# New order lists for the five engines of an adaLN block with infini-attention, on one core

## The chip, the cores and the metric

The kernel runs on one core of a Trainium2 chip. Its engines work side by side: TensorE (PE) multiplies matrices, VectorE (DVE) and ScalarE (ACT) work on tiles and read what PE leaves in PSUM, GpSimd (POOL) works on tiles in SBUF, SyncE (SP) issues nearly all transfers. The metric is the device time of one execution in microseconds (us), the median of several runs. Lower is better. The kernel before runs in 747.37 us (median of 3 runs, 746.82 to 749.26).

## What is computed

The block is a transformer layer in float32 over 2048 positions of width 512: a layer norm modulated by a condition vector, causal attention over four segments of 512 positions with 32 heads of 16, mixed by a gate with a linear memory that is carried from segment to segment, an output projection, a second modulated layer norm, and a dense layer of 1792 with the square of a ReLU.

```python
phi = lambda t: jnp.where(t > 0, t + 1.0, jnp.exp(t))
for s in range(N):                       # 4 segments of 512
    logits = jnp.einsum("bhqd,bhkd->bhqk", qs, ks) * scale + mask
    p = _softmax(logits, axis=-1)
    a_dot = jnp.einsum("bhqk,bhkd->bhqd", p, vs)
    pq = phi(qs)
    num = jnp.einsum("bhld,bhde->bhle", pq, M)
    den = jnp.einsum("bhld,bhd->bhl", pq, z)[..., None] + 1e-6
    o = g * num / den + (1.0 - g) * a_dot
    pk = phi(ks)
    M = M + jnp.einsum("bhld,bhle->bhde", pk, vs)
    z = z + jnp.einsum("bhld->bhd", pk)
...
mod = (_silu(c) @ w_mod).reshape(c.shape[0], 6, 1, -1)
sa, ca, ga, sb, cb, gb = (mod[:, 0], mod[:, 1], mod[:, 2], mod[:, 3], mod[:, 4], mod[:, 5])
h = _layernorm(x, axis=-1) * (1 + ca) + sa
x = x + ga * _A_ref(h, ...)              # attention and the projection wo
h = _layernorm(x, axis=-1) * (1 + cb) + sb
r = relu(h @ w1 + b1)
x = x + gb * ((r * r) @ w2 + b2)
```

## The kernel before

Matrices are held as a high part and a rest, so that a product of float32 accuracy is three products of the faster type. The attention is cut into 16 units: unit u is segment u // 4 and a group of 8 heads, u % 4; each unit is worked in two quads of four heads.

For a unit, PE first makes queries and keys (bqk, L868), and for a segment the values (bv, L938). ACT and DVE split queries and keys in two parts (sg, L899 and L901), and SP copies the parts into the buffer ST by many small transfers, the fills (L917). For each quad PE then makes masked scores (ba, L976) of which DVE takes the row maxima (mx, L981; one reduction, L1020, goes by a copy ac of ACT, L1009). PE turns the maxima (bat, L1041), ACT negates them (mt, L1043), and SP writes them as a further row into ST (two transfers, L1049). Only then can PE make the scores less their maximum (bpb, L1145); ACT takes the exponentials (pt, L1162), POOL masks them, PE multiplies them with the values (bpv, L1204), and at the end of a unit PE turns the results (bfin) and DVE divides them in two halves, each of three instructions (L1253 to L1256, result on). The memory is read on PE (bmr, L1069) and brought up to date by way of bmu and tm (L1106, L1121).

At the end of the attention the blocks of the output weights wo are loaded (L1297, four of 256 KB), multiplied by the gate on DVE (L1298), cast to their high part on ACT (L1299) and split on DVE (L1300). They land in the place of the value weights, so the loads wait for the last value product. The projection starts with a transposition (bwot, L1332).

The dense layer runs both of its products as seven block products each (L1652 the first, L1737 the second). In the first pass p counts pairs of 128-column blocks of w1 and s the segment; its operands come from a transformed w1 in HBM (w1d0 to w1d6) by fetches (L1579) into buffers that the products of an earlier p release.

Nothing of the order is left to a scheduler. The program makes a list of nodes (a node is one step on one engine: a group of matmuls, one copy, one or two transfers), each with its inputs and the buffers that it takes and gives back. `Plan.run` then plays the nodes through a model with a duration for each, and issues them in the order that comes out. On each engine it takes them in the order of a table of node numbers, `ORDER`. PSUM's eight banks and most tiles come from pools in that same play: a node takes the bank that has been free for longest, so another order also changes which earlier user's release a node waits for.

Of the kernel before, what the change touches and what calls it, by code (L numbers as in the profile page):

```python
# [69 lines left out]
1208 1499 1240 1500-1501 1236 1144 1248 1503-1504 1331 1243 1505 1220 1506 1325 1481 1338 1482 1346 1483 1560 1328  # L70
1484 1322 1252-1254 1256 1259 1486 1349 1487 1263 1488 1334 1489 1343 1617 1352 1618 1515 1619-1620 1523 1271 1266
1622-1623 1529 1624 1355 1625 1275-1277 1520 1752 1368 1753 1279 1371 1754 1536 1755 1544 2043 2039 1375 1757 1557
1378 1758 1526 1759 1383 1760 1547 2047 2035 1387 1550 1532 1388 1563 1389 1541 1650 1692 1391 1887 1398 1888 1401
1889 1394 1655 1890 1664 1406 1892 1410 1661 1566 1893 1569 1894 1553 1895 1658 1671 1411-1412 1676 1573 1576 1685
1695 1585 1682 1581 1586 1589 1827 1667 1587 1592 1698 1596 1679 1599 1414 1604 1608 1785 1790 1701 1609 1830 1793
1704 1610 1708 2051 1711 2052 1799 1716 2053 1688 2054 1806 1820 1612 1720 1833 1721-1722 1724 1814 2056 1727 2057
1796 1731 2058 1734 1962 1739 2059 1817 1802 1743-1745 1920 1811 2080-2081 1928 1836 1823 2082 1934 2083 1843 1747
2085 1851 2086 1846 2087-2088 1925 1839 2209-2210 1931 2156 1941 2211-2212 1949 1937 1855-1857 1859 1955 2214 2114
2215 1952 2216 1965 2217 2119 1862 2097-2099 1866 2100 1869 1946 2102 1874 2103 2125 1958 2104 2135 2146 2105 2149
1878 496 1879-1880 1971 2128 2333 1974 2334 1978 2140 2335 2122 2336 1981 1882 2338 1986 2339 2143 2340 2131 2341 2259  # L80
498 1990 2273 1994 1991-1992 1997 2457 2270 2001 2458 2004 2459 2152 2264 2460 2280 2238 2462 2267 2463 2009 2464 2246
2465 2243 2013-2014 2249 2159 2015 2162 2166 2169 2017 1968 2178 2276 2174 2252 2599 2362 2182 2179-2180 2185 2404
2602-2603 2189 2604 2376 2605 2192 2197 2607-2608 2255 2609-2610 2373 2633 2616 2201 2383 2367 2202-2203 2283 2370
2619 2286 2620-2622 2290 2298 2379 2624-2625 2205 2486 2626-2627 2293 2650 2302 2500 2636-2639 2397 2306 2303 2641
2309 2642 2497 2643-2644 2653-2654 2394 2655-2656 2491 2667 2304 2658 2313 2659-2660 2316 2661 2670-2671 2321 2388
2672-2673 2684 2407 2675-2676 2410 2677-2678 2391 2325-2327 2494 2414 2687 2417 2688-2689 2400 2690 2701 2422 2692
2507 2693-2695 2512 2781 2769 2430 2503 2426 2433 2515 2437 2427-2428 2521 2440 2704 2445 2705-2706 2531 2707 2518
2777 2773 2718 2449-2451 2538 2524 2709-2711 2534 2721 2712 2722 2541 2723-2724 2453 2546 2726-2729 2554 2557 2550
2329 2561 2564 2551 2528 2569 2552 2573-2575 2973 2577 2977 2972 2828 2817 2974-2975 2831-2833 2976 2834 2820 2839
2821-2822 2978 2823 2842-2843 2994 2806 2844 2993 2845 2996 2995 2850 2998-2999 2809 2997 2810-2812 2853 2861  # L90
2854-2856 3014-3015 3122 2864 3016 2883 3017 2865-2867 3314 3018 2886 3019 2887 2872 3020 2888-2889 3035-3036 3038
3037 2875-2878 3041 3040 3120 3119 3121 3039 3329 3054 3133 3131 3319 3055 3143 3134 3056 3324 3057 3146 3132 3060
3059 3058 3144 3074-3075 3073 3145 3078 3076 3079 3158 3077 3155 3092 3094-3095 3093 3157 3098 3097 3167 3156 3170
# [1742 lines left out]
```

## Time and profile before

| | before |
|---|---|
| runs | 747.37 us (746.82 to 749.26) |
| profiled execution | 746.45 us |
| its span | 744.7 us |
| TensorE busy | 724.5 us |
| VectorE busy | 623.7 us |
| GpSimd busy | 495.5 us |
| ScalarE busy | 485.7 us |
| transfers over the span | 151.82 MB, mean 204 GB/s |

The profile is one execution. Its span runs from the first instruction to the last; the execution's own time is 1.75 us longer. "Busy" is the time in which an engine has an instruction in work. In rows of waits, the name left of the arrow is the instruction that stood idle, and the one to the right released it. A row of a timeline starts with the start and the duration in us, joins neighbours of one kind (x2, x12), and puts an idle time ahead of it in brackets. SPq is SP's queue of transfers: its rows show how long the issue took, not the transfer. PEclk is the granted clock of TensorE, 1.00 being full speed.

### The profile page before, as it was taken

Reading aid. Unit: us, or ns where it says so; the run is one execution under the profiler, and the core shown is the slowest. Engines: PE = TensorE matmul, PEld = TensorE weight load, DVE = VectorE, ACT = ScalarE, POOL = GpSimd, SP = SyncE. Lnnn points to the kernel's source line nnn. Section 1 sums busy time; section 2 is a strip of 40 time slices with the busy share of each in tenths; the row PEclk is TensorE's granted clock in tenths of the full one; section 3 lists DMA queues with packets and bytes.
Section 4 is the critical chain, followed back from the end, with each engine's and each line's share of the span. In section 5 each row is a group of like instructions: output and inputs, shape, how many; then the busy total and the mean of one; then the engine's idle time right before and its main releaser. Section 6 shows DMA issues by size and latency. Waiting matters only on the chain. (4 is left out here: it accounts for less than half of the span.)

```text
span 744.7 us, 20355 instructions
## 1 busy us (share of the span) xinstructions
PE 724.5 (97%) x7405; PEld 612.3 (82%) x7405; DVE 623.7 (84%) x1674; ACT 485.7 (65%) x1070; POOL 495.5 (67%) x675
## 2 busy tenths in 40 slices
PE   8989999999999999998999999999999999999996
PEld 7876778666767677784777788999999999999996
DVE  6578898898898889888998879789788888777785
ACT  3759887999979987787779645574435443534342
POOL 6767857789858786553996656656666665466572
PEclk9999999999999999999999999999999999999999
DMA  9877874545644363438762897898876678776620
GB/s 310 259 212 236 236 198 115 154 121 165 193 145 121 94 184 96 124 98 270 252 207 88 232 358 255 301 330 290 288 234 218 225 256 263 261 237 223 195 83 29
DMA packets 84606, 151.82 MB, mean 204 GB/s; under 512 B 10134, under 2 KB 32666, under 8 KB 84508
## 3 DMA queue, kind: packets, MB, share of 16 engines
q1 hardware_dynamic: 84356, 150.40, 64.4%
q8 instruction: 59, 0.97, 0.5%
q14 instruction: 39, 0.32, 0.1%
q10 hardware_dynamic: 152, 0.13, 0.1%
HBM read 94.14 MB, written 29.36 MB: 166 GB/s over the span
## 5 line engine op out<-in xcount | busy, mean ns | idle before, releaser
L981 DVE CUSTOM_DVE_ANT_0 ba<-ba,msk 128x384 f32<-128x384 f32 (+2 forms) x384 | 192.9, 531 | 26.9 <-PE ba L976 19.8
L1162 ACT ACTIVATE pt<-bpb 128x512 f32<-128x512 f32 x320 | 173.4, 618 | 10.3 <-PE bpb L1145 8.8
L1149 POOL TENSOR_SCALAR_AFFINE_SELECT pt<-pt 128x512 f32<-128x512 f32 x128 | 80.3, 646 | 52.8 <-ACT pt L1162 38.4
L868 PE MATMUL bqk<-HT,WQK 64*128 64x512 f32 x720 | 105.2, 396 | 0.4 <-ACT HT L844 0.3
L1737 PE MATMUL bm<-w,ST 128*128 128x256 f32 x660 | 93.5, 283 | 0.5 <-DVE ST L1725 0.4
L1737 PEld LDWEIGHTS bm<-w,ST 128*128 128x128 f32 x660 | 85.0, 191 | 1.1 <-DVE ST L1725 1.1
L1652 PE MATMUL bh<-ST 128*128 128x256 f32 x600 | 84.4, 283 | 1.1 <-DMA ST<-w1d 1.1
L1145 PE MATMUL bpb<-ST 64*128 64x256 f32 (+2 forms) x512 | 79.5, 349 | 3.1 <-DMA ST<-mt 2.4
L1204 PE MATMUL bpv<-pt,VT 128*32 128x512 f32 (+3 forms) x1024 | 82.0, 438 | 0.3 <-ACT lnf L657 0.2
L1652 PEld LDWEIGHTS bh<-ST 128*128 128x128 f32 x600 | 77.1, 190 | 2.0 <-ACT H2o L1443 1.3
L868 PEld LDWEIGHTS bqk<-HT,WQK 64*128 64x128 f32 x720 | 70.4, 185 | 9.5 <-ACT VT L944 0.8
L976 PE MATMUL ba<-ST 63*128 63x256 f32 (+2 forms) x512 | 75.2, 341 | 2.0 <-DVE on L1256 1.3
L976 PEld LDWEIGHTS ba<-ST 63*128 63x128 f32 x512 | 50.1, 185 | 21.9 <-DVE mx L981 2.6
L1145 PEld LDWEIGHTS bpb<-ST 64*128 64x128 f32 x512 | 51.6, 188 | 19.9 <-DVE mx L981 3.1
L938 PE MATMUL bv<-WVO,HT 64*128 64x512 f32 x384 | 54.8, 399 | 0.0
L1204 PEld LDWEIGHTS bpv<-pt,VT 128*32 128x32 f32 x1024 | 27.1, 109 | 33.5 <-issue 26.5
L981 DVE DVE_READ_ACCUMULATOR2_ANT mx<- 128x1 f32 x384 | 54.2, 141 | 0.1
L910 POOL TENSOR_SCALAR e<-e 128x512 f32<-128x512 f32 x24 | 35.8, 1493 | 16.4 <-ACT e L906 16.2
L938 PEld LDWEIGHTS bv<-WVO,HT 64*128 64x128 f32 x384 | 38.0, 188 | 4.3
L1009 ACT COPY ac<-ba 128x512 f32<-128x512 f32 x64 | 36.2, 604 | 7.0 <-PE ba L976 6.2
L779 POOL TENSOR_TENSOR X1L<-X1L 128x512 fp32r<-128x512 f32 (+1 forms) x28 | 32.2, 1149 | 12.4 <-ACT X1L L778 12.0
L1020 DVE TENSOR_REDUCE mx<-ac 128x4 f32<-128x1024 f32 x32 | 38.9, 1215 | 0.3 <-POOL ac L1017 0.2
(291 smaller groups left out, 1719.7 us busy)
## 6 DMA issues: line engine op xcount, KB each, us to landing
ST<-sg SPq DMA_DIRECT2D x192, 128.0 KB
ST<-w1d SPq DMA_DIRECT2D x20, 1024.0 KB
ST<-w1d SPq DMA_DIRECT2D x20, 768.0 KB
w1d<-X1L SPq DMA_DIRECT2D x21, 512.0 KB
w1c<-w1d SPq DMA_DIRECT2D x8, 1024.0 KB
w1c<-w1d SPq DMA_DIRECT2D x8, 768.0 KB
xt<-in_A_x SPq DMA_DIRECT2D x16, 256.0 KB
wm<-in_w_mod SPq DMA_DIRECT2D x16, 256.0 KB
```

Source lines behind the costliest of these rows:

```text
L868: nc.tensor.matmul(bank(banks[w]), W3(w, k, x, cols.start, cols.stop)[r], HT[r, y, k], start=first and i == 0, stop=last and i == 2)
L938: nc.tensor.matmul(bank(banks[t]), HT[r, x, k, (t2 + t) * P:(t2 + t + 1) * P], WVO[r, k, y], start=first and i == 0, stop=last and i == 2)
L976: nc.tensor.matmul(dst[:, c0:c0 + n], ST[b:b + 63, 0, sl, qt * P:(qt + 1) * P], ST[b:b + 63, 1, sl, :n], start=True, stop=True)
L981: nc.vector.tensor_tensor_reduce(i, i, msk[:, 512 - n:], scale=1.0, scalar=-3e38, op0=ALU.add, op1=ALU.max, accum_out=o)
L1009: cp = [act(512, lambda j=j: nc.scalar.copy(buf("ac", ac)[:, j], bank(keys[j])), pr[0] + 0.01 + 0.001 * j, after=[first], put=[keys[j]]) f ...
L1020: reds.append(op("DVE", 1.13, lambda: nc.vector.tensor_reduce(buf("mx", mx).rearrange("p (a t) -> p a t", t=4)[:, :, 1], acv(), axis=AX.X, ...
L1145: nc.tensor.matmul(dst, ST[b:b + 64, 1, sl, kb * P:(kb + 1) * P], ST[b:b + 64, 0, sl, q0:512], start=True, stop=True)
L1149: nc.gpsimd.affine_select(out=ap, in_=ap, pattern=[[0, ap.shape[1]], [1, P]], compare_op=ALU.is_ge, fill=0.0, base=0, channel_multiplier=-1)
L1162: ns = [op("ACT", 0.49, lambda j=j: nc.scalar.activation(buf("PPP"[n], pt)[:, i + j], bank(keys[j]), AF.Exp, scale=0.25), pr[slot] + 0.01 ...
L1204: nc.tensor.matmul(bank(o)[32 * hq:32 * hq + 32, q0:q0 + src.shape[1]], v[:, a:a + 32], src, start=start, stop=stop, tile_position=(0, 32 ...
L1652: nc.tensor.matmul(pb(i), A[:, x, kk], B[:, y, kk], start=kk == j == 0, stop=kk == 1 and j == 2)
L1737: nc.tensor.matmul(q if wide else q[:, c * HALF:(c + 1) * HALF], TL[ao][a >= 3][:, x, a_ * P:(a_ + 1) * P], LT["w2z"][:, b:15:14 - b] if w ...
```

## The change

Only the table `ORDER` is different: the five lists hold the same node numbers (1309 for PE, 1054 for ACT, 984 for DVE, 617 for POOL, 499 for SP) in another order, found by a search, stretch by stretch, over six draws of durations, transfer landings and queue rate. No node, duration, pool or line of code is changed besides. The first lines of PE's list stand for all:

```diff
     "PE": """
-8-24 3 25-33 56 34-37 58 64 38-39 82 78 66 90 40-43 86 44-47 252 246-249 253-255 405-408 410-413 291-293 308 294 322
-564-565 319 296 316 297 566 313 567 298-299 329 569-570 337 571 325 572 340 274-275 334 276-277 350 355 279 362 365
...
+8-24 3 25-33 56 34-37 58 64 38-39 82 78 66 90 40-43 86 44-47 252-253 246-247 254 248-249 255 405-408 410 291 411-413
+292-293 308 322 294 564-565 316 296 313 297 566-567 319 298-299 329 569-570 337 325 571-572 340 274-277 334 350 355
...
```

Three places show what that moves. The first is the head of the attention, the first row of maxima of unit 0. SP's list before, from the two clears of ST (L749) to the transfers of that row (L1049); wm is a load of the modulation's weights:

```order
L781 DMA w1d_131<-X1L 256x2x256
L917 DMA ST<-sg 32x2x512 x3
L749 DMA ST<-pad 32x4x512 x2
L917 DMA ST<-sg 32x2x512
L590 DMA wm<-in_w_mod 128x512
L917 DMA ST<-sg 32x2x512
L1049 DMA ST<-mt 1x8x128 x2
L917 DMA ST<-sg 32x2x512
```

and now:

```order
L781 DMA w1d_131<-X1L 256x2x256
L917 DMA ST<-sg 32x2x512 x3
L749 DMA ST<-pad 32x4x512 x2
L917 DMA ST<-sg 32x2x512
L1049 DMA ST<-mt 1x8x128 x2
L917 DMA ST<-sg 32x2x512
L781 DMA w1d_131<-X1L 256x1x256
L917 DMA ST<-sg 32x2x512 x6
```

The load of w_mod and one fill between the clears and the row have gone behind it. On PE the same place before, from the masked scores (ba) to the first scores (bpb); the number behind ba is its bank's tile:

```order
L976 MATMUL ba_643<-ST 128x384
L976 MATMUL ba_644<-ST 128x384
L868 MATMUL bqk<-HT,WQK 128x512 x6
L1041 MATMUL bat<-ident,mx 16x64 x2
L868 MATMUL bqk<-HT,WQK 128x512 x6
L976 MATMUL ba_683<-ST 128x512
L976 MATMUL ba_684<-ST 128x512
L938 MATMUL bv<-WVO,HT 128x512 x12
L976 MATMUL ba_711<-ST 128x512
L976 MATMUL ba_712<-ST 128x512
L938 MATMUL bv<-WVO,HT 128x512 x12
L1094 MATMUL bpkt<-ident,phi_469 128x64 x8
L1145 MATMUL bpb<-ST 128x512 x2
```

and now:

```order
L976 MATMUL ba_645<-ST 128x384
L976 MATMUL ba_646<-ST 128x384
L1041 MATMUL bat<-ident,mx 16x64 x2
L868 MATMUL bqk<-HT,WQK 128x512 x12
L976 MATMUL ba_682<-ST 128x512
L976 MATMUL ba_683<-ST 128x512
L938 MATMUL bv<-WVO,HT 128x512 x24
L976 MATMUL ba_733<-ST 128x512
L976 MATMUL ba_734<-ST 128x512
L1094 MATMUL bpkt<-ident,phi_411 128x64 x8
L1145 MATMUL bpb<-ST 128x512 x2
```

The transposition of the maxima (bat) stands ahead of one group of six products of bqk that was ahead of it before, and one pair of masked scores has moved behind all the value products.

The second place is the scaling of the output weights, in units 11 to 14. DVE before (numbers tell the tiles apart; wo_6304, wo_6321 and wo_6329 are the first three blocks in the order of their loads, bfin and on belong to unit 11, tm to its memory):

```order
L1020 TENSOR_REDUCE mx_6281<-ac_6220 128x4
L1298 TENSOR_TENSOR wo_6329<-wo_6329,gab_6082 128x512
L1121 TENSOR_TENSOR tm_6423<-bmu_6397,bdm_101 128x34
L1298 TENSOR_TENSOR wo_6321<-wo_6321,gab_6082 128x512
L1253 RECIPROCAL bfin_6373<-bfin_6373 128x16
L1255 TENSOR_TENSOR dn_6434<-bfin_6373,omg_77 128x16
L1256 TENSOR_TENSOR on_6437<-bfin_6373,dn_6434 128x4x64
L1253 RECIPROCAL bfin_6375<-bfin_6375 128x16
L1255 TENSOR_TENSOR dn_6448<-bfin_6375,omg_77 128x16
L1256 TENSOR_TENSOR on_6437<-bfin_6375,dn_6448 128x4x64
L1298 TENSOR_TENSOR wo_6304<-wo_6304,gab_6082 128x512
```

and now (the first three blocks loaded are wo_6293, wo_6306 and wo_6321):

```order
L1298 TENSOR_TENSOR wo_6293<-wo_6293,gab_6076 128x512
L1298 TENSOR_TENSOR wo_6306<-wo_6306,gab_6076 128x512
L1253 RECIPROCAL bfin_6368<-bfin_6368 128x16
L1255 TENSOR_TENSOR dn_6400<-bfin_6368,omg_77 128x16
L1256 TENSOR_TENSOR on_6403<-bfin_6368,dn_6400 128x4x64
L1298 TENSOR_TENSOR wo_6321<-wo_6321,gab_6076 128x512
L1121 TENSOR_TENSOR tm_6434<-bmu_6406,bdm_101 128x34
L1020 TENSOR_REDUCE mx_6283<-ac_6222 128x4
L1253 RECIPROCAL bfin_6366<-bfin_6366 128x16
L1255 TENSOR_TENSOR dn_6461<-bfin_6366,omg_77 128x16
L1256 TENSOR_TENSOR on_6403<-bfin_6366,dn_6461 128x4x64
```

Two scalings and one half of a unit's end stand ahead of tm now, and the reduction, which was ahead of all, has moved behind tm. SP before, from the fills ahead of the loads on:

```order
L1049 DMA ST<-mt 1x8x128 x2
L917 DMA ST<-sg 32x2x512 x6
L1297 DMA wo<-in_A_wo 128x512
L1522 DMA T_6297<-gb_dram 128x512
L1297 DMA wo<-in_A_wo 128x512 x2
L917 DMA ST<-sg 32x2x512
L1321 DMA ot<-o_dram 128x512
L1322 DMA xw<-in_A_x 128x512
L917 DMA ST<-sg 32x2x512 x4
L1297 DMA wo<-in_A_wo 128x512
```

and now:

```order
L1049 DMA ST<-mt 1x8x128 x2
L917 DMA ST<-sg 32x2x512 x4
L1297 DMA wo<-in_A_wo 128x512 x3
L1321 DMA ot<-o_dram 128x512
L1322 DMA xw<-in_A_x 128x512
L917 DMA ST<-sg 32x2x512 x2
L1297 DMA wo<-in_A_wo 128x512
```

The first three loads of wo follow one another, with four fills instead of six between them and the row of maxima ahead, and the load T<-gb_dram is no longer among them. Of the fills of unit 14, eight instead of seven stand ahead of the loads in all.

The third place is the end of the dense layer's first pass over segment 0. SP before; w1d_136 and w1d_137 are the blocks for p = 5 and p = 6, L1374 stores rows of the sum behind the attention, L1690 partial sums of the dense layer, L1693 loads such sums again:

```order
L1579 DMA ST<-w1d_136 128x2x1024
L1693 DMA Tx_7999<-xs_146 128x512
L1579 DMA ST<-w1d_136 128x2x768
L1579 DMA w1c<-w1d_137 128x2x1024
L1690 DMA xs_148<-T_6297 128x512
L1374 DMA x_dram<-Tx_8001 128x512
L1579 DMA ST<-w1d_137 128x2x768
L1579 DMA ST<-w1d_131 128x2x1024
```

and now:

```order
L1579 DMA ST<-w1d_136 128x2x1024
L1374 DMA x_dram<-T_6303 128x512
L1579 DMA ST<-w1d_136 128x2x768
L1579 DMA w1c<-w1d_137 128x2x1024
L1374 DMA x_dram<-X1L 128x512
L1579 DMA ST<-w1d_137 128x2x768
L1579 DMA ST<-w1d_131 128x2x1024
L1596 DMA w_8795<-w2d_144 128x1792
```

A store (L1690) has moved from between the fetches of p = 6 to behind them, a load (L1693) from between those of p = 5. PE before, the products of p = 5 (six to a group) from the first that reads the second half's operands:

```order
L1737 MATMUL bm<-w_7992,ST 128x256 x6
L1652 MATMUL bh<-H2o_6295,ST 128x256 x6
L1652 MATMUL bh<-ST 128x256 x6
L1652 MATMUL bh<-H2o_6294,ST 128x256 x6
L1737 MATMUL bm<-w_7992,ST 128x256 x6
L1652 MATMUL bh<-ST 128x256 x18
L1737 MATMUL bm<-w_7993,ao 128x256 x3
L1652 MATMUL bh<-ST 128x256 x6
```

and now:

```order
L1737 MATMUL bm<-w_7999,ST 128x256 x9
L1652 MATMUL bh<-H2o_6301,ST 128x256 x6
L1652 MATMUL bh<-H2o_6300,ST 128x256 x6
L1652 MATMUL bh<-ST 128x256 x24
L1737 MATMUL bm<-w_7999,ST 128x256 x6
L1652 MATMUL bh<-ST 128x256 x6
```

Four groups now stand together (x24) where three stood behind two groups of the second product (bm); the last reader of the buffer that the fetch for p = 6 takes is the second of the four, before the second of the three.

More of the change, by code (lines that the diff above doesn't have):

```diff
@@ new lines @@
+1346 1483 1560 1328 1484 1322 1252-1254 1349 1256 1486-1487 1334 1259 1488 1263 1343 1489 1617 1352 1618 1515
+1619-1620 1271 1266 1523 1622-1624 1355 1529 1625 1520 1275-1277 1752 1368 1753 1279 1371 1754 1536 1755 1544 2039
+2043 1375 1757 1557 1378 1758 1526 1759 1383 1760 1547 2035 2047 1387 1550 1532 1388 1563 1389 1541 1650 1692 1391
+1887 1398 1888 1401 1889 1394 1655 1890 1664 1406 1892 1410 1661 1566 1893 1569 1894 1553 1895 1658 1671 1411-1412
+1676 1573 1576 1685 1695 1585 1682 1581 1586 1589 1827 1667 1587 1592 1679 1596 1698 1599 1604 1414 1608 1785 1790
@@ new lines @@
+3243 3257 3410 3425 3424 3427 3258 3426 3704 3256 3255 3267 3429 3270 3268-3269 3428 3430 3442 3444 3282 3443 3699
+3279 3445 3291 3294 3280 3446 3281 3447 3292 3448 3460 3507 3293 3709 3714 3463 3461-3462 3504-3505 3466 3506 3478
+3464-3465 3519 3516 3479-3481 3518 3517 3483 3482 3531 3529 3484 3528 3530 3543 3542 3751 3541 3540 3553 3750 3555
+3554 3552 3749 3752 3567 3755 3565 3564 3754 3566 3576 3578 3769 3753 3577 3770 3579 3775 3771 3773 3772 3605-3607
+3774 3604 3619 3616-3618 3790 3628 3631 3629 3789 3630 3791 3641 3794 3793 3642 3640 3795 3792 3643 3809 3655
@@ new lines @@
+2432 2505 2770 2434 2438 2435 2439 2429 2441-2442 2447 2446 2532 2708 2778 2774 2533 2719 2452 2525-2526 2540 2539
+2536 2535 2542 2793 2725 2543 2548 2547 2789 2555 2559 2558 2556 2791 2562 2565 2563 2566 2571 2570 2798 2553 2576
+2787 2795 2979 2829 2818 2800 2840 2807 2987 2989-2990 2988 3000 2851 3115 2905 2952 2901 3117 3315 2954 2903
+3010-3011 3021 2862 2914 2884 2916 2918 3127 3031 2873 3129 3042 3032 2929 2927 3052-3053 3029 2931 3030 3325 3139
+3141 3061 3330 3320 3008 3050-3051 3151 3153 3071-3072 3080 2942 2940 2944 3069 3099 3335 3163 3009 3165 3337
@@ new lines @@
+1656 1666 1665 1663 1662 1660 1659 1678 1677 1897 1686-1687 1903 1683-1684 1675 1829 1828 1681 1699 1680 1415-1416
+1792 1791 1795 1794 1789 1800-1801 1614 1613 1821 1834 1822 1815-1816 1798 1797 1810 1964 1963 2061 1819 2067 1818
+1812-1813 1929-1930 1936 1935 1748 1924 1749 1926-1927 1932-1933 2157-2158 1950 1945 1951 1956-1957 1954 1953
+2120-2121 2219 1947 2225 1948 2118 2126-2127 2150 2147 2151 2148 2139 2130 2129 2142 2141 2123 1883 2124 1884
+2144-2145 2343 2274 2349 2275 2271-2272 2263 2265-2266 2281-2282 2269 2268 2247 2245 2248 2244 2467 2251 2473 2250
```

331 lines of the change are left out of this document (157 added, 174 removed), and 9 rows, old and new, of the table ORDER.

## Prediction

> **What bounds the kernel now.** I read the page's busy table first, then the waits of PE, then windows around them.
>
> ```profile
> span 744.7 us, 20355 instructions
> PE 724.5 (97%) x7405; PEld 612.3 (82%) x7405; DVE 623.7 (84%) x1674; ACT 485.7 (65%) x1070; POOL 495.5 (67%) x675
> ```
>
> PE is the bound: it is idle for only 744.7 − 724.5 = 20.2 us. The change adds no work and removes none, so all it can win is idle time of PE, and what the clock loses after an idle stretch. The waits of PE (what it waited for, us in total, how often, longest) say where that time lies:
>
> ```profile
> PE bpb L1145 <- DMA ST<-mt: 2.4, 1, 2.4
> PE bwarm L570 <- POOL ident masks.py:199: 1.9, 1, 1.9
> PE bh L1652 <- DMA ST<-w1d: 1.4, 2, 1.1
> PE bat L1041 <- DVE tm L1121: 1.4, 1, 1.4
> PE ba L976 <- DVE on L1256: 1.3, 1, 1.3
> PE bmr L1069 <- ACT ac L1009: 1.1, 1, 1.1
> ```
>
> Apart from the start (bwarm, 1.9), five single waits hold 2.4 + 1.1 + 1.4 + 1.3 + 1.1 = 7.3 us. These I followed through the new lists. The windows show what surrounds them:
>
> ```profile
> core 0: us, PE busy (x) PEld busy (x) DVE busy (x) ACT busy (x) POOL busy (x), PEclk, DMA share, GB/s
> 46.24:49.65 3.41, 1.23 (x18) 0.94 (x14) 3.41 (x9) 1.92 (x5) 1.55 (x3) 1.00 0.38 110
> 49.65:53.06 3.41, 3.17 (x18) 3.20 (x20) 0.96 (x2) 1.64 (x3) 0.00 (x0) 0.50 0.82 227
> 343.00:346.41 3.41, 2.04 (x49) 0.90 (x46) 1.67 (x4) 2.60 (x7) 1.59 (x3) 1.00 1.00 362
> 150.00:175.00 25.00, 24.20 (x322) 15.00 (x320) 23.79 (x83) 24.83 (x57) 21.30 (x27) 1.00 0.49 136
> 725.00:745.00 20.00, 13.16 (x106) 12.55 (x104) 11.57 (x20) 5.29 (x10) 6.07 (x8) 0.94 0.08 27
> ```
>
> The first two rows belong together: PE idles through most of 46.24 to 49.65, and the next 3.41 us run at a granted clock of 0.50. The third holds waits as well, 2.04 us of work, and the full clock. The last is the end: PE is idle there for 6.84 us behind the final sums on DVE, whose number the lists leave alone; some are swapped, which I cost at nothing, since all of them must be done before the last store. Named waits, start and end make 7.3 + 1.9 + 6.8 = 16.0 us; the remaining 4.2 lie thinly over the span.
>
> **The head: the row of maxima, 47.5 to 49.9.** The first score group (bpb) needs a row with the negated maxima. Its way is a transposition on PE (bat), two copies on ACT (mt), two DMAs on SP. SP's, ACT's and PE's timelines (start, duration) in turn:
>
> ```profile
> 42.25 1.23 SPq L917 DMA_DIRECT2D ST<-sg  x1
> 43.58 1.22 SPq L590 DMA_DIRECT2D wm<-in_w_mod  x1
> 44.84 0.61 SPq L917 DMA_DIRECT2D ST<-sg  x1
> 45.54 2.40 SPq L1049 DMA_DIRECT2D ST<-mt  x2
> ```
>
> ```profile
> 43.26 0.32 ACT L1043 ACTIVATE mt<-bat 16x64 fp32r<-16x64 f32 x2
> ```
>
> ```profile
> 45.66 1.57 PE L938 MATMUL bv<-WVO,HT 64*128 64x512 f32 x12
> 47.05 0.42 PE L1094 MATMUL bpkt<-ident,phi 64*128 64x64 f32 x8
> 49.89 0.97 PE L1145 MATMUL bpb<-ST 64*128 64x512 f32 x2 [2.42 <-DMA ST<-mt]
> 50.45 1.69 PE L938 MATMUL bv<-WVO,HT 64*128 64x512 f32 x6
> ```
>
> The copies end at 43.58, but SP is busy until 45.45 with a load of w_mod and a fill; then both DMAs take 2.40 us to issue, and PE starts 49.89 − 47.94 = 1.95 us after the second. In the new lists that load and one fill stand behind the row's DMAs, and bat stands one group of six products earlier, so that the copies come earlier too. Two DMA issues fewer ahead, at the unhindered 0.61 us of the row at 44.84, are 1.2 us; at most it is 45.54 − 43.58 = 1.96, if the slow 1.22 goes altogether and the copies are early enough. At least it is nothing, if the queue that held up the load holds up the row instead. I take 1.2 (the unhindered issues): the wait falls from 2.42 to 1.2. The groups that PE does between bat and the score are the same but for the one that bat overtakes, so nothing else is late there; the load moved behind is one of the modulation's, whose products come far later. **−1.2 us (0 to −2.0).**
>
> The clock follows from it. The window ahead of the drop held 1.23 us of PE work in 3.41; with 1.2 us less waiting it holds 2.4, and the window at 343 with 2.04 kept the full clock. So I take the drop to go. Its price: 3.17 us of work at half the clock. Six products take 1.69 us there, twelve take 1.57 at full clock, so about half of it, 1.6, is lost; a little of that was bound by weight loads, so 1.5. **−1.5 us (0 to −1.6).** [...]
>
> **The scaled output weights, 344 to 353.** Three waits of PE stand close together. SP's timeline, DVE's, PE's, and the DMA rate between 336 and 346:
>
> ```profile
> 337.42 0.59 SPq L1297 DMA_DIRECT2D wo<-in_A_wo  x1
> 338.12 0.36 SPq L1522 DMA_DIRECT2D T<-gb_dram  x1
> 338.53 0.91 SPq L1297 DMA_DIRECT2D wo<-in_A_wo  x2
> ```
>
> ```profile
> 342.17 1.22 DVE L1020 TENSOR_REDUCE mx<-ac 128x4 f32<-128x1024 f32 x1
> 345.12 0.69 DVE L1298 TENSOR_TENSOR wo<-wo,gab 128x512 f32<-128x512 f32 x1 [1.74 <-DMA wo<-in_A_wo]
> 345.74 0.18 DVE L1121 TENSOR_TENSOR tm<-bmu,bdm 128x34 f32<-128x34 f32 x1
> 345.84 1.01 DVE L1298 TENSOR_TENSOR wo<-wo,gab 128x512 f32<-128x512 f32 x1
> ```
>
> ```profile
> 345.98 0.22 PE L1041 MATMUL bat<-ident,mx 64*16 64x64 f32 x1 [1.37 <-DVE tm L1121]
> 345.98 0.51 PE L1145 MATMUL bpb<-ST 64*128 64x256 f32 x4
> 347.75 0.56 PE L976 MATMUL ba<-ST 63*128 63x256 f32 x4 [1.26 <-DVE on L1256]
> ...
> 352.57 1.17 PE L1069 MATMUL bmr<-MB,phi 64*128 64x68 f32 x16 [1.07 <-ACT ac L1009]
> ```
>
> ```profile
> DMA packets 1460, 2.56 MB, mean 256 GB/s; under 512 B 215, under 2 KB 215, under 8 KB 1459
> ```
>
> DVE scales a weight block that has not landed, and what stands behind it (tm, the ends of an attention unit) holds the PSUM banks for which bat and ba wait. That block was the third of its kind issued, at about 339.0, behind two other blocks and the load at 338.12. In the new list the three blocks follow one another, that load is far behind, and the block that DVE needs second is the second. They cannot be issued before 337.4: the last value product must have read what they overwrite, and it stands one place later on PE. So the issue comes 1.1 us earlier (337.9), and 384 KB less stand ahead (two transfers of 256 KB fewer, one fill of 128 more): at 256 GB/s 1.5 us. These are two views of the same backlog; I take 1.5, landing at 343.6 (bounds: 345.1, if the fills fill the room; 342.5, if both add up).
>
> DVE's new queue is two scalings, one end, a third scaling, tm, the reduction (1.22, no longer ahead of the scaling, which costs nothing as DVE would only wait), the other end. With 0.6 to 0.7 for a scaling, 0.9 for an end (346.85 to the release at 347.75) and 0.1 for tm: second scaling done at 344.3, end 345.2, tm 345.95, reduction 347.1, other end 348.0. The banks pass to other holders. Bat waits for the first end, 345.2 instead of 345.98; the score group behind it now waits for tm and ends at 346.45, as before; ba takes banks that ACT has long released, and starts at 346.4 instead of 347.75; the group behind the next transposition waits for the other end, 348.0, and gives some back; bmr waits for an exponential that now stands behind two casts of the weights on ACT, for about 351.4 instead of 352.57. **−1.15 us (+0.3 with landing at 345.1, −2.3 with 342.5).** Queued behind the two scalings are both ends, tm and the reduction, and PE waits for all four: from a landing at 344.8 on this place costs more than before, a microsecond for each microsecond.
>
> **The last weight fetch of the first FFN pass, 485 to 493.** SP's timeline and PE's:
>
> ```profile
> 485.62 2.32 SPq L1579 DMA_DIRECT2D ST<-w1d  x2
> ```
>
> ```profile
> 492.80 1.43 PE L1652 MATMUL bh<-ST 128*128 128x256 f32 x10 [1.14 <-DMA ST<-w1d]
> ```
>
> The fetch waits for the last product that reads its buffer. That product stands three groups earlier now, and the group that needs the fetch stands where it stood. Ten products take 1.43 us here, so a group of six some 0.86 and three groups 2.6, less what they overlap: the fetch is issued about 2 us earlier, more than the 1.14 of the wait; on SP a store between the fetches (L1690) has moved behind them. **−1.1 us (0 to −1.14).**
>
> **What the rest costs.** Like rows side by side are one row in a printed order: PE has 1690 of them instead of 1684, so about six changes of shape more. The trace has no row for a change; twelve products take 1.57 us from start to end while 45.66 to 47.05, start to start, is 1.39, so that groups overlap by about 0.2, and a change costs between nothing and that. I take 0.08, nearer to nothing, since most neighbours in these timelines overlap whatever their shape: **+0.5 (0 to +1.2).** Everything else moves by one to three places, above all the two halves of a pair; the cover is PE's queue, 97% full, and buffers that stay the same in number. Without that cover, each late release costs about what those waits cost, 1.1 to 1.4.
>
> **The sum** against the profiled execution: 746.45 − 1.2 − 1.5 − 1.15 − 1.1 + 0.5 = 742.0. That execution lies 0.92 below the median of the runs, 747.37, so the runs should show **742.9**.
>
> **Rivals.**
> [...]
> - *The gains are taken up.* The queue holds up the row anyway (0 to −0.5 instead of −1.2), so the clock drops, and the weights land at 345 (+0.3). With −0.5 + 0.3 − 1.1 + 0.5 that is 745.65, or 746.6 in the runs: no measurable change. For it: the DMA share of 1.00 in the window at 343, and the 1.22 us that SP needed for one issue at 42 to 45, where the queue was the limit, not SP's list.
> - *Slower: ACT loses turns between 150 and 175.* There ACT is busy for 24.83 of 25 us and paces PE; its list has exponentials, copies of masked scores and layernorm casts in a new order, with two copies moved behind five others. If what now stands first isn't ready, ACT idles, nothing covers it, and PE's banks stay held. A turn there is 24.83 us for 57 instructions, 0.44. The gains of 4.45 are gone at ten lost turns; from (4.45 + 2.24) / 0.44 = 15 of the 57 on the kernel is slower by over 0.3%: about 750. Against it: in that window most entries are swaps of two halves whose inputs one PE group makes, and PE itself is 24.20 busy.
> - *More goes than named.* Half of the thinly spread 4.2 us goes as well: 740.8.
>
> **How the numbers follow.** 0.3%, about what a measurement can tell from no change, is 2.24 us: faster means below 745.1, slower above 749.6. Forecast 0.42, the clock still drops 0.12, more than named 0.12: faster 0.66. Taken up: 0.22. ACT loses turns: 0.12. The range must leave out no more than a fifth: it leaves out most of the slower rival and a little at the low end. Low: 742.9 with the head at its bound (−0.8), the weights at theirs (−1.15) and half the spread idle time (−2.1) would be 738.9; not all at once, so 739.5. High: the gains taken up and the changes of shape at their bound (+0.7), 747.3, and a lost turn or two: 748.3.
>
> **What would show it.** In the new profile the wait of bpb for mt should be near 1.2 us, and the granted clock in 50 to 75 should be 1.00. DVE's wait for wo should be gone or end by about 344 in before's time, and no PE wait over 1 us stand between bat and bmr. The fetch should leave no wait of bh. If the head's wait is still over 2 us, the queue and not SP's list set it, and the sum loses 2.7. If ACT's idle time between 150 and 175 grows by some us, the slower rival holds.

## The result, and the profile after

The changed kernel ran in 743.5 us (median of 5 runs, 740.82 to 744.21), the kernel before beside it in 748.49 (5 runs, 746.82 to 750.35): a ratio of 0.9929, 95% interval 0.9902 to 0.9956, about 5 us faster. (Ratios in this text are those that came with the runs; the quotient of the medians can differ a little, here 0.9933.) The profiled execution took 743.41 us, only 3.0 less than the profiled execution of before (746.45); that one was quicker than most of its kind, as the experiments show.

The page of the changed kernel, its span and its engines:

```profile
span 741.6 us, 20354 instructions
PE 725.6 (98%) x7405; PEld 615.6 (83%) x7405; DVE 623.1 (84%) x1674; ACT 485.2 (65%) x1070; POOL 493.3 (67%) x675
```

PE has the same 7405 instructions and is still the bound; its idle time went from 20.2 to 741.6 − 725.6 = 16.0 us. Its waits (what it waited for, us in total, times, longest):

```profile
PE bwarm L570 <- POOL ident masks.py:199: 1.9, 1, 1.9
PE blnq L653 <- ACT pt L1162: 1.1, 1, 1.1
PE bh L1652 <- DMA ST<-w1d: 1.0, 1, 1.0
PE bwop L1355 <- ACT oraw L1228: 0.8, 2, 0.5
PE bpb L1145 <- DMA ST<-mt: 0.6, 1, 0.6
```

The three waits at 344 to 353 (bat for tm, ba for on, bmr for ac) are gone from the list, and the one of bpb for the row of maxima fell from 2.4 to 0.6. The wait of bh for a fetch is not the old one, as shown below. The 1.1 of blnq, near 58 us, is new; in E12, the changed kernel once more, it is not there. The windows of the changed kernel, columns as in the prediction:

```profile
46.24:49.65 3.41, 2.79 (x31) 2.68 (x29) 3.28 (x9) 2.55 (x7) 2.60 (x4) 1.00 0.57 165
49.65:53.06 3.41, 3.16 (x33) 2.75 (x30) 2.77 (x10) 3.02 (x8) 1.97 (x2) 1.00 0.57 132
150.00:175.00 25.00, 24.68 (x323) 15.04 (x321) 23.42 (x84) 23.99 (x56) 23.82 (x31) 1.00 0.51 144
425.00:450.00 25.00, 23.67 (x147) 20.57 (x146) 18.08 (x36) 11.48 (x22) 14.73 (x20) 1.00 0.94 299
```

The half clock behind the head's wait is gone: 2.79 us of work where there were 1.23, then 1.00 instead of 0.50. At 150 to 175 PE is busier than before (24.68 against 24.20). New is the fourth row: at 425 to 450 PE idles for 1.33 us.

**Head.** SP's and PE's timelines (start, duration, idle time in brackets):

```profile
43.20 1.49 SPq L917 DMA_DIRECT2D ST<-sg  x1
44.78 1.98 SPq L1049 DMA_DIRECT2D ST<-mt  x2
...
48.38 0.65 PE L1145 MATMUL bpb<-ST 64*128 64x512 f32 x2 [0.62 <-DMA ST<-mt]
```

The row is issued right behind one fill, and PE starts at 48.38 instead of 49.89.

**Output weights.** SP's, DVE's and PE's timelines:

```profile
336.57 2.61 SPq L1297 DMA_DIRECT2D wo<-in_A_wo  x3
...
341.29 1.29 DVE L1298 TENSOR_TENSOR wo<-wo,gab 128x512 f32<-128x512 f32 x2
344.00 0.18 DVE L1121 TENSOR_TENSOR tm<-bmu,bdm 128x34 f32<-128x34 f32 x1
...
344.12 0.22 PE L1041 MATMUL bat<-ident,mx 64*16 64x64 f32 x2
349.33 1.11 PE L1069 MATMUL bmr<-MB,phi 64*128 64x68 f32 x16
```

DVE scales two blocks at 341.29 without any wait, and neither bat nor bmr has a bracket.

**Last fetch of the first FFN pass, and a new wait before it:**

```profile
482.49 3.40 SPq L1579 DMA_DIRECT2D ST<-w1d  x2
...
433.22 0.96 PE L1652 MATMUL bh<-H2o,ST 128*128 128x256 f32 x6 [0.96 <-DMA ST<-w1d]
```

The fetch goes out 3.1 us earlier than at 485.62 (1.0 of that is the lead that PE has there), and no wait is left near 491. The 0.96 us at 433.22 had no counterpart before.

**Tail.** The last PE group and the last DVE sum, before and then after:

```profile
737.93 0.52 PE L1737 MATMUL bm<-w,ao 128*128 128x256 f32 x3
741.13 0.41 DVE L1771 TENSOR_TENSOR T<-T,bm 128x256 f32<-128x256 f32 x1
```

```profile
734.63 0.52 PE L1737 MATMUL bm<-w,ao 128*128 128x256 f32 x3
738.10 0.41 DVE L1771 TENSOR_TENSOR Tx<-Tx,bm 128x256 f32<-128x256 f32 x1
```

The last sum starts 3.20 us behind PE's last group before, 3.47 after; the span ends 6.77 us behind it before, 6.97 after.

### The profile page after: what moved, and what is told of

It is laid out like the page before. It is cut to its first block, busy times and chain, and to the rows that moved or that the text cites. A ratio compares the mean times of both kernels' runs of the same rounds, so it can differ in the third digit from the quotient of the medians.

```text
span 741.6 us, 20354 instructions
## 1 busy us (share of the span) xinstructions
PE 725.6 (98%) x7405; PEld 615.6 (83%) x7405; DVE 623.1 (84%) x1674; ACT 485.2 (65%) x1070; POOL 493.3 (67%) x675
## 4 chain that ended last, share of the span: by engine, by line
PE 85%; DVE 5%; DMA 3%; ACT 3%; issue 1%; POOL 1%; SPq 1%; DVEq 0%; ACTq 0%; POOLq 0%
PE bm L1737 18%; PE bh L1652 18%; PE bqk L868 11%; PE bpv L1204 8%; PE ba L976 6%; PE bpb L1145 6%; PE bv L938 5%; PE bwop L1355 2%; PE bwarm L570 2%; DVE ba L981 1%; DMA ST<-w1d 1%; PE bmr L1069 1%; PE blnq L644 1%; PE blnq L653 1%; DMA ST<-sg 1%
## 5 line engine op out<-in xcount | busy, mean ns | idle before, releaser
L1145 PE MATMUL bpb<-ST 64*128 64x256 f32 (+2 forms) x512 | 81.5, 347 | 0.7 <-DMA ST<-mt 0.6
L868 PEld LDWEIGHTS bqk<-HT,WQK 64*128 64x128 f32 x720 | 73.4, 185 | 8.6 <-ACT HT L844 0.8
L976 PE MATMUL ba<-ST 63*128 63x256 f32 (+2 forms) x512 | 77.3, 341 | 0.9 <-DMA ST<-sg 0.6
L976 PEld LDWEIGHTS ba<-ST 63*128 63x128 f32 x512 | 52.5, 185 | 20.6 <-issue 4.6
L1145 PEld LDWEIGHTS bpb<-ST 64*128 64x128 f32 x512 | 53.6, 185 | 16.5 <-issue 3.9
L1020 DVE TENSOR_REDUCE mx<-ac 128x4 f32<-128x1024 f32 x32 | 38.9, 1214 | 0.1
L1652 PE MATMUL bh<-H2o,ST 128*128 128x256 f32 x252 | 35.7, 281 | 1.4 <-DMA ST<-w1d 1.0
```

Source lines behind the costliest of these rows:

```text
L868: nc.tensor.matmul(bank(banks[w]), W3(w, k, x, cols.start, cols.stop)[r], HT[r, y, k], start=first and i == 0, stop=last and i == 2)
L976: nc.tensor.matmul(dst[:, c0:c0 + n], ST[b:b + 63, 0, sl, qt * P:(qt + 1) * P], ST[b:b + 63, 1, sl, :n], start=True, stop=True)
L1020: reds.append(op("DVE", 1.13, lambda: nc.vector.tensor_reduce(buf("mx", mx).rearrange("p (a t) -> p a t", t=4)[:, :, 1], acv(), axis=AX.X, ...
L1145: nc.tensor.matmul(dst, ST[b:b + 64, 1, sl, kb * P:(kb + 1) * P], ST[b:b + 64, 0, sl, q0:512], start=True, stop=True)
L1652: nc.tensor.matmul(pb(i), A[:, x, kk], B[:, y, kk], start=kk == j == 0, stop=kk == 1 and j == 2)
```

## The experiments

All kernels compute the whole block and differ only in `ORDER`. The runs of before that went with them give medians of 749.43 (16 runs, for the first four kernels below that were run: E1, E2, E3, E4), 747.88 (13, for E5 to E8) and 748.35 (35, for E9 to E12). Each of these three groups ran on a chip of its own, so that a ratio compares with the runs of before in the same group. Single runs of before lie between 744.5 and 753.5, so that kernels run once are read by their rows, not by their time. In some kernels the lists take fewer lines of text, and line numbers are 4 or 5 lower. "Lead" is the start of a product in PE's list against the start of the product with the same number in the first profile of before, since PE runs 7405 of them in each (negative: earlier).

### E1: the kernel before, profiled once more

No edit.

> The order lists of before, unchanged, for a second profile. If the three places are waits of the order itself, they stand again: bpb on the row of maxima 2.4 us and the half clock after it, bat, ba and bmr at 344 to 353 together 3.7, bh on the weight fetch near 491 1.1, and PE's groups start within 0.5 us of the first profile's times up to the end. If they are chances of one execution, single ones are missing and PE's times differ by 1 us and more.

One run, 750.58 us. PE's timeline at the head, and windows at the output weights:

```profile
51.10 0.68 PE L1145 MATMUL bpb<-ST 64*128 64x512 f32 x2 [2.50 <-DMA ST<-mt]
...
348.00:352.00 4.00, 2.73 (x18) 1.90 (x14) 3.83 (x13) 3.29 (x9) 1.67 (x2) 0.67 0.90 310
352.00:356.00 4.00, 4.00 (x34) 1.76 (x34) 4.00 (x8) 2.23 (x5) 0.00 (x0) 0.50 0.91 305
```

The waits at the head and near 491 stand again, 2.5 and 1.2; at 344 to 353 two of the three do (bat 0.9, ba 1.3, no bmr). PE is 2.1 us late at 94 and 4.1 at the end, so the times do not repeat within the 0.5 us that was expected of an order alone. And there is a second place at half clock, for 6.8 us from 349.4 on, among the waits there. The first profile had not shown it: of six profiles with before's lists at this place five have it. The prediction priced one drop; these profiles usually have two.

### E2: only the row of maxima moved, on SP

```diff
 DMA ST<-sg 32x2x512
-DMA wm<-in_w_mod 128x512
-DMA ST<-sg 32x2x512
 DMA ST<-mt 1x8x128 x2
-DMA ST<-sg 32x2x512
+DMA wm<-in_w_mod 128x512
+DMA ST<-sg 32x2x512 x2
```

> Before, with one node of SP's list moved: the row of maxima of the first quad ahead of the load of w_mod and the fill that stood ahead of it. Theory 1, SP's list sets the wait: the row is issued 1.2 to 2.0 us earlier, the wait of bpb falls from 2.4 to 0.4 to 1.2, the clock stays at 1.00, and PE is 2.7 to 3.4 us earlier from 55 us on. Theory 2, the backlog of the queue sets it: the row's own issue takes longer instead, the wait stays above 2, and the half clock stands again: less than 0.5 us. Theory 3, the transposition's earlier place on PE is needed as well: the row cannot be issued before its copies end at 43.6, so the wait falls by at most 1.9 even so.

One run, 747.0. SP issues the row at 44.19 (45.54 before), and PE's timeline shows the shorter wait, with no half clock behind it:

```profile
48.92 0.69 PE L1140 MATMUL bpb<-ST 64*128 64x512 f32 x2 [1.04 <-DMA ST<-mt]
```

The wait falls by 1.4, and at 52.8 us the lead is −2.25 (in E1 +0.18). What the two DMAs do to the issue shows in every profile: counted from the start of the clears, the row is issued after 4.5 to 4.9 us in the seven with before's head, and after 2.6 to 2.9 in the five with two DMAs fewer (this one, the changed kernel twice, E3, E4). How much of the wait follows is less sure: E9 below has a wait of 1.03 with the old list.

### E3: before with the head's new order on all engines, and E9: the changed kernel with the old head

E3 takes the new order up to about 50 us, E9 takes it everywhere but there. SP's list in E3 against before:

```diff
-DMA ST<-sg 32x2x512 x7
+DMA xt<-in_A_x 128x512 x3
+DMA ST<-sg 32x2x512 x6
...
 DMA ST<-sg 32x2x512
-DMA wm<-in_w_mod 128x512
-DMA ST<-sg 32x2x512
 DMA ST<-mt 1x8x128 x2
```

> Before, with the order of the changed kernel on all five engines up to some 50 us, and the order of before from there on. If the head's gain is its own: PE 2.9 us earlier at 55 us, as in the changed kernel, and, if nothing behind takes it back, still 2 to 3 us earlier at the end: 0.3 to 0.4% faster. Rival, the gain is taken up by the stretches where ACT or DVE pace PE (75 to 200): PE is less than 1.5 us earlier from 200 us on, and the time within 0.2% of before.

> The changed kernel with the order of before on all five engines up to some 52 us: the counterpart of the run with the head alone (ratio to before 0.9966). If the gains of the places add up, the ratio is the changed kernel's 0.9929 less the head's share, 0.995 to 0.998, and PE gains 1.8 to 2.3 us at 344 to 353 and 1 to 1.5 us net between 423 and 520. If the head's gain is mostly taken back behind it, as in the stretch from 60 to 340 of the changed kernel, this run is as fast as the changed kernel: 0.993.

E3: 746.9 us (11 runs), ratio 0.9966, interval 0.9947 to 0.9984. E9: 744.52 us (10 runs), ratio 0.9933, interval 0.9909 to 0.9958. Their profiles are the odd ones out. E3's SP and PE, then E9's:

```profile
46.70 2.11 SPq L1045 DMA_DIRECT2D ST<-mt  x2
...
51.66 0.97 PE L1141 MATMUL bpb<-ST 64*128 64x512 f32 x2 [3.69 <-DMA ST<-mt]
```

```profile
46.73 1.52 SPq L1049 DMA_DIRECT2D ST<-mt  x2
...
49.34 0.68 PE L1145 MATMUL bpb<-ST 64*128 64x512 f32 x2 [1.03 <-DMA ST<-mt]
```

With the new head, E3's execution had SP two microseconds late already at the clears of ST (44.01 against 41.89 in the changed kernel), a wait of 3.69 and two stretches at half clock; with the old head, E9's had a wait of 1.03 and none, since the row was there 1.09 us behind its issue instead of 1.95. So the size of this wait belongs to the execution as much as to the order, and one profile of each kernel can't price it; the runs can. They show that the head alone is worth 0.34%, some 2.5 us, and that leaving it out of the whole change costs nothing that these runs resolve: 0.9933 with the old head, 0.9929 and (E12) 0.9941 with the new one. The product 0.9966 × 0.9933 = 0.990 lies just below both intervals of the changed kernel, and has one of its own of some ±0.003: that the parts fall short of adding up is likely, not certain.

### E5 and E6: the output weights, by SP's list alone and by DVE's alone

E5 is before with the new order of SP between 319 and 354 us only, E6 with that of DVE only:

```diff
 SP (E5)
-DMA wo<-in_A_wo 128x512
-DMA T<-gb_dram 128x512
-DMA wo<-in_A_wo 128x512 x2
+DMA wo<-in_A_wo 128x512 x3
 DVE (E6)
-TENSOR_REDUCE mx<-ac 128x4
+TENSOR_TENSOR wo<-wo,gab 128x512 x2
```

> Before, with SP's list of the changed kernel between some 319 and 354 us (three loads of wo in a row, the load T<-gb_dram behind them, four fills instead of six ahead); all other lists as before. Theory 1, the landing of the loads decides at 344 to 353: DVE no longer waits for wo (1.7 before), the wait of bat (1.4) goes, ba and bmr wait less than 0.7 each, and PE gains 1.5 to 2.5 us there. Theory 2, the order on DVE and the banks decide: DVE scales earlier, but tm and the ends stand where they stood, and PE gains less than 0.7.

> Before, with DVE's list of the changed kernel between some 319 and 354 us (two scalings of wo and one end of a unit ahead of tm, the reduction behind it); SP's and all other lists as before. Theory 1 (the slower mechanism of the prediction): the loads still land at 345, DVE waits 2.5 us or more for them with both ends, tm and the reduction behind, and PE loses 0.3 to 1.5 us at 344 to 353. Theory 2, the order on DVE brings the gain: PE gains 1 us or more.

One run each, 749.78 and 750.78. DVE's and PE's timelines in E5:

```profile
344.61 1.22 DVE L1020 TENSOR_REDUCE mx<-ac 128x4 f32<-128x1024 f32 x1
345.74 0.68 DVE L1298 TENSOR_TENSOR wo<-wo,gab 128x512 f32<-128x512 f32 x1
...
352.67 1.17 PE L1069 MATMUL bmr<-MB,phi 64*128 64x68 f32 x16 [0.20 <-ACT ac L1009]
```

DVE goes from the reduction to the scaling without a stop, the waits of bat and ba are gone, bmr's is 0.20 instead of 1.07; PE gains 2.36 us between 339 and 354, and there is no half clock. (E5 then loses 3.8 us between 363 and 423, in waits for POOL and for fills at 367 to 392 that before does not have: the other lists no longer fit SP's.) DVE's timeline in E6:

```profile
345.16 1.43 DVE L1298 TENSOR_TENSOR wo<-wo,gab 128x512 f32<-128x512 f32 x2 [0.81 <-DMA wo<-in_A_wo]
```

The wait for the load is still there, though 0.81 and not the 2.5 that was expected, and PE loses 1.0 us between 339 and 354 (the other profiles with before's order there: from 1.3 lost to 0.5 gained). So the gain comes from the landing of the loads, and DVE's turns alone bring none.

### E7 and E8: the last fetch, and the stretch around it

E7 is before with one group of PE moved, the last reader of the fetch's buffer; E8 is before with the new order of all engines from 461 to 522.

```diff
 MATMUL bh<-H2o,ST 128x256 x6
+MATMUL bh<-ST 128x256 x6
 MATMUL bm<-w,ST 128x256 x6
-MATMUL bh<-ST 128x256 x18
+MATMUL bh<-ST 128x256 x12
```

> Before, with one group of PE's list moved: the product of p = 5 that last reads the buffer for the fetch of p = 6 stands two groups earlier, ahead of the group of the second product (bm). Theory 1, that release alone sets the wait of bh near 491: the fetch is issued 1.4 us earlier, and the wait of 1.1 goes: PE 1.0 to 1.2 us earlier from 495 us on. Theory 2, the transfer is paced by the queue: it lands at the same time, and the wait stays above 0.8.

> Before, with the changed kernel's order on all five engines between some 461 and 522 us, the stretch in which the changed kernel's lead grows by 3.05 us (0.6 at 490, 3.66 at 520). Theory 1, the gain is this stretch's own: PE is 2.5 to 3 us earlier at 520, and the kernel 0.3 to 0.4% faster. Theory 2, the stretch only takes back what the changed kernel lost between 423 and 463 (1.8 us; the fetches pace both kernels): PE is 1.0 to 1.5 us earlier at 520, the 1.1 of the wait for the fetch and some tenths.

E7: one run, 748.62. No wait near 491 is left, and PE gains 1.37 us between 490 and 505: the one moved group does it. E8: 747.12 us (10 runs), ratio 1.0001, interval 0.9982 to 1.002. PE gains 2.07 us between 490 and 520, of which 0.4 were lost on the way there from 463. (The 3.05 of the expectation sets groups of unequal size against each other; by the count of products the changed kernel gains 2.33 there.) The time doesn't show it: a gain of 2 us would be 0.9973, outside that interval. The 1.25 us that its own profile keeps from 463 to PE's last group would be 0.9983, just inside. Alone, this place is worth nothing that these runs resolve.

### E4: the changed kernel with the old order from 416 to 439

It asks whether the new waits there (433.22 above) are worth mending.

```diff
-DMA W2s<-in_B_w 128x2x512
 DMA W2s<-gb_dram 128x512
 DMA ST<-w1d 128x2x1024
+DMA W2s<-in_B_w 128x2x512
+DMA Tx<-in_A_x 128x512
+DMA Tx<-o_dram 128x512
...
 DMA ST<-w1d 128x2x1024
-DMA x_dram<-T 128x512 x2
-DMA T<-o_dram 128x512
```

> The changed kernel, with the order of before on all five engines between some 416 and 439 us (from the last attention unit to the first products of the dense layer), where the changed kernel loses 1.8 us of its lead (2.3 us ahead at 423, 0.5 at 436). Theory 1, the new order there makes the waits of bh for weight fetches: they go, PE is again 2 to 2.5 us ahead at 440, and the kernel is 1 to 2 us faster than the changed one. Theory 2, the transfers there are the limit whatever the order (DMA share 0.94 in 425 to 450): PE loses the lead there all the same, and the time is that of the changed kernel.

744.42 us (6 runs), ratio 0.9938, interval 0.992 to 0.9956: as the change. The lead at 436 is kept (−1.92 instead of −0.51), but it is gone by 480 (−0.13, and −1.00 in the changed kernel), and part of it goes in this row:

```profile
446.56 0.74 PE L1732 MATMUL bm<-w2a,ST 128*128 128x256 f32 x4 [0.97 <-DVE ST L1720]
```

What is saved at one wait is taken up by the next.

### E10 and E11: the row still earlier, and a version to beat both

E10 is the changed kernel with the row of maxima ahead of the remaining fill and one more load of w_mod behind; E11 is E10 with before's order from 416 to 474.

```diff
-DMA ST<-sg 32x2x512
-DMA ST<-mt 1x8x128 x2
-DMA ST<-sg 32x2x512
+DMA ST<-mt 1x8x128 x2
+DMA ST<-sg 32x2x512 x2
 DMA w1d<-X1L 256x1x256
```

> The changed kernel with two nodes of SP's list moved: the first row of maxima ahead of the fill that still stood ahead of it, and one load of w_mod behind the fills that follow. Theory 1, the place of SP in its list against PE sets the wait, and SP runs up to 2 us later or earlier from one execution to the next: the row is issued about 1.5 us earlier relative to the clears than in the changed kernel, the wait of bpb (0.6, 1.1 and 3.7 in three profiles with this head) is under 0.5 or, in a late execution, 2 or less; the median falls by 0.5 to 1.5 us against the changed kernel. Theory 2, the row's transfers are slow themselves: they take as much longer, and neither wait nor median changes.

> As the run before, and with the order of before on all five engines between some 416 and 474 us, since the changed kernel and its version with the order of before up to 439 both lose 1.8 to 2.0 us by 463, each in another place. Theory 1, the new order of that stretch makes the fetches late wherever it begins: PE keeps its lead over before to 470 and still gains 2 to 3 us between 480 and 520; 3 us faster than the changed kernel at most, 1 us at least. Theory 2, being earlier at 423 is itself what runs into the fetches: the lead goes again, and the time is that of the run before.

E10: 743.74 us (12 runs), ratio 0.9941, interval 0.9919 to 0.9963; E11: 743.94 (12 runs), ratio 0.9952, interval 0.9927 to 0.9978. Neither beats the changed kernel. In E10 SP and PE show

```profile
43.23 2.20 SPq L1049 DMA_DIRECT2D ST<-mt  x2
...
47.57 0.48 PE L1145 MATMUL bpb<-ST 64*128 64x512 f32 x1
```

no wait at all, and at 52.8 us a lead of −3.42. At 329 it is −0.42, less than in the changed kernel (−0.85). E11 keeps more at 436 (−1.37) and ends no earlier (span 741.9).

### E12: the changed kernel once more

No edit.

> The order lists of the changed kernel, unchanged, for a second profile and times beside those of this job. The places at 344 to 353 and the fetch near 491 should be without waits over 0.7 us as in its first profile; the wait of bpb at the head between 0.3 and 3.7, since SP's pace varies; ratio to before 0.990 to 0.996.

743.38 us (10 runs), ratio 0.9941, interval 0.9914 to 0.9969. In its profile the head's wait is twice that of the first, and still without half clock; the old waits at 344 to 353 and at 491 are gone again, and the new one near 433 stands (1.15):

```profile
49.45 0.68 PE L1145 MATMUL bpb<-ST 64*128 64x512 f32 x2 [1.40 <-DMA ST<-mt]
```

## Why the prediction came out as it did

It said 742.9, and the kernel ran in 743.5 and 743.4. It was right in sign and size, and the three places that it followed (row of maxima, output weights, last fetch) are those where the profiles gain. But its errors cancel: one gain was half of what came, another was put at the wrong place, and the losses between the places were put at nothing. That the sum hit within a microsecond is in part luck. The table gives, in us, the change of the lead over each stretch of PE's list: as predicted, in the first two profiles, and as the mean of the profiles with the new order (the changed kernel twice, E4, E9, E10, E11) against the mean of those with the old (before twice, E2, E3, E5 to E8). A profile is left out where its own edit touches a stretch or could still act in it.

| stretch (before's time) | predicted | first pair | means |
|---|---|---|---|
| 16 to 94: the head's wait, and the clock | −2.7 | −2.6 | −3.0 |
| 94 to 329 | 0 | +1.25 | +0.8 |
| 329 to 363: output weights | −1.15 | −2.3 | −2.5 |
| 363 to 423 | 0 | +0.8 | +0.4 |
| 423 to 490 | 0 | +1.4 | +1.7 |
| 490 to 520: last fetch | −1.1 | −2.3 | −2.0 |
| 520 to PE's last group | 0 | 0.0 | −1.0 |
| from there to the end | 0 | +0.2 | +0.2 |

With the changes of shape (+0.5) the prediction comes to −4.45. The first pair comes to −3.55, and to the −3.1 of the spans with the 0.5 us by which the changed kernel's execution was later at 16 us already; the means come to some −5.3, near the −5.0 of the runs.

**The head's wait (−1.2): right in what SP's list does, its size left to chance.** The two DMAs set when the row is issued, in every profile (E2). But the wait is 2.06 to 2.74 in six of seven profiles with the old list (for the 2.74, in E8, the profile names a reduction on DVE, L1020, as the releaser) and 1.03 in the other (E9); with the new one it is 0.56 (E4), 0.62 and 1.40 (the changed kernel) and 3.69 (E3). The rival "the gains are taken up" is half true here: of the lead, 0.8 us is given back by 329 in the mean, more where the row came earliest (E10 2.0, E11 2.3), and by E9 the whole change needs no new head, as far as its runs resolve it. ACT, busy for 24 of 25 us at 150 to 175, may pace that stretch; no run shows it.

**The clock (−1.5): the drop at the head went in the profiles, but what the runs gain in clock comes from elsewhere.** Each run has a mean granted clock: in the profiled ones it is 0.997 to 0.999 where no stretch of 3.4 us was at half clock, 0.996 or 0.997 with one, 0.993 with two (E6, E8) and 0.991 with three (E1, E3, E7, where two follow each other at one place). Of the 35 last runs of before 22 are at 0.996 or below, of 45 runs with the new order (the changed kernel, E4, E10, E11, E12) 3. The head's order is not what does it. E3, with the new head and the old rest, has a mean clock of 0.9951 over 11 runs, before beside it 0.9942 over 16; E9, with the old head and the new rest, has 0.9980 over 10, E12 with both new 0.9975 over 10. So the term is at the wrong place, as far as the runs tell: their clock rises with the rest of the order, and the only other place where a profile shows half clock between the start and the last sums is 347 to 360, at the output weights. The prediction's one profile had no drop there, and the prediction had no term for it. What a stretch costs a run stays open: by an estimate from clock and time of single runs (a stretch lowers the mean clock by some 0.0023) it is 0.4, 0.3 and 0.9 us in the three groups of runs of before, each uncertain by some 0.3 to 0.4, and 1.9 in E3's runs, uncertain by 0.5.

**The output weights (−1.15): right in cause, half the size.** The step that was off is the landing at 343.6. The three loads left at 336.57, which with the lead of 0.9 is the 337.4 of the prediction, and were there before DVE asked at 341.29 (342.2 in before's time), at or under its early bound of 342.5, which gave −2.3. That fits loads and fills that add up, where the prediction took the middle. What this place is worth in the time of a run was not measured alone: E5 has the waits gone and loses their gain again by 423. That E9 keeps the whole gain without the head, and that E8 shows none, points to it.

**The last fetch (−1.1): right in cause and size, with more beside it.** From 490 to 500 us the lead grows by 1.39 in the first pair, and by 1.37 in E7 from the one moved group. Another 0.9 comes by 517, at two places where before's PE waits for DVE and neither the changed kernel's nor E8's does; the prediction had nothing for them. Before's rows:

```profile
508.70 0.74 PE L1737 MATMUL bm<-w,ST 128*128 128x256 f32 x4 [0.19 <-DVE ST L1725]
...
514.82 1.06 PE L1737 MATMUL bm<-w2a,ST 128*128 128x512 f32 x6 [0.24 <-DVE X1L L1773]
```

What the prediction had at nothing, 423 to 490, costs 1.7: its cover, "PE's queue, 97% full", is not there at 433, where a fetch is 0.96 us late. Mending that wait is no cure, as E4 shows, which has lost 1.8 of its lead between 436 and 480. From 423 to 520 the gain is 1.0 in the first pair and 0.3 in the means, where 1.1 was predicted.

**The tail (0): +0.2.** "All of them must be done before the last store" was too quick: the last sum begins 0.27 later behind PE's last group, and the span ends 0.2 later behind it. (The window 725:745 reaches 0.3 us past the span's end, so the idle time at the end is 6.5 and the unnamed rest 4.5; no term of the sum hangs on it.) **Changes of shape (+0.5)** can't be told apart from all this.

**The step to the runs (+0.92)** was too small: before's profiled execution lies 1.9 us under the median of its 35 later runs, 748.35. The predicted gain of 4.45 was half a microsecond short of the 5.0 measured, and the base was a microsecond too low. **The slower rival** fell: at 150 to 175 ACT is busy for 0.84 us less than before, but PE for 0.48 more.

## What to carry to other kernels

When an order changes, follow each named wait to the transfer that releases it: moving the transfer's issue earlier did the work here (E2, E5, E7), moving the engine that waits for it did not (E6). Don't count on gains of places to add up: the head won 2.5 us alone and nothing that the runs resolve on top of the rest (2.5 us would be at the edge of what they resolve), and the last fetch's stretch 2.1 us in its profile and nothing that its runs resolve. A lead can be spent in the waits that come next, as between 94 and 329 and between 423 and 490. And look at two or three executions before pricing a wait that hangs on the queue of transfers, since one may show a drop of the clock and the next not; the mean clock of many runs tells where the drops went.

## What the runs showed of the hardware

- **The pace of a queue differs between executions.** Seven kernels have the same lists up to the row of maxima (before, E1, E5 to E9), and yet SP issued it at 45.54 in before, 46.71 in E1, 47.38 in E5; PE started 1.95 us behind the end of the issue in before, E1, E6 and E7, 1.09 behind it in E5 and E9 (2.72 in E8, where the profile names another releaser). What decides between the two was not found.
- **The clock fell behind waits of 2.06 us and more, and mostly behind shorter ones close together.** Waits of 2.06 to 3.69 us at the head were followed by 3.4 us or twice that at 0.50 in all seven profiles that have them (before, E1, E3, E5 to E8); none of 0.56 to 1.40 was. At 344 to 353 two or three waits of 0.8 to 1.9 us within some 7 us were followed by half clock in five of six (E1, E2, E3, E7 and E8, not before). By the trace's record of the granted clock, the stretch in before lasts 3.413 us and begins at 49.65, 13 times that behind the record's start at 5.28; at the end of the changed kernel one begins at 740.13, 215 times behind the start at 6.27. In E1, E3, E6 and E8 the two places lie 297 or 304 us apart, read off the clock of windows around them, which is 87 or 89 times 3.413. Two windows of E2 and one of E12, which kept its clock:

```profile
344.48:347.89 3.41, 1.86 (x17) 1.30 (x19) 3.27 (x10) 2.79 (x7) 2.29 (x3) 1.00 0.92 310
347.89:351.30 3.41, 3.41 (x32) 1.24 (x30) 3.38 (x10) 2.69 (x6) 0.00 (x0) 0.50 0.97 318
...
48.00:51.41 3.41, 2.01 (x19) 1.90 (x19) 2.73 (x6) 1.73 (x4) 1.15 (x2) 1.00 0.58 156
```

E2 lost the clock behind 1.86 us of work in 3.41, before at the head behind 1.23; E12 kept it with 2.01, and before kept it at 344 to 353, with 1.95, 2.24 and 2.34 us of work in the three windows of 3.41 from 343.17 to 353.40. In E6 it fell at 355.8, where 352 to 356 held 2.56 us of work in 4.00. What decides between the two was not found.
- **At half clock six products took 1.69 us, where twelve took 1.57 at full clock (before, at the head).** From these two rows the prediction estimated a loss of 1.5 on the 3.17 us of work in that stretch. How much of that a run loses is not settled by these runs (estimates from 0.3 to 1.9 us, above).
